# Attention and two feed-forwards on one core: part of the gate products moved to VectorE, weight jobs in other slots, and a new order of the prologue

## The chip, the cores and the metric

The kernel runs on one core of a Trainium2 chip. A core has TensorE (PE, matrix products; PEld is its weight load), VectorE (DVE), ScalarE (ACT), GpSimd (POOL) and SyncE (SP), each with an instruction stream of its own, run in order; a stream stands still where an instruction waits for a semaphore. Matrix products land in PSUM banks, 128 partitions by 512 float32; all other tiles lie in SBUF. Transfers are issued by SP, ACT or POOL and carried by 16 DMA engines. The metric is the device time of one launch in microseconds (us), the median of several runs.

## The reference

Batch 4, 8 heads, 576 tokens, head size 64. Two attentions are added: one over tokens averaged by four (144 by 144, repeated back to 576), one over a band in which positions differ by under four. Their sum, 2304 tokens by 512 channels, goes through two feed-forwards:

```python
out_up = np.repeat(sm_attn(q_d, k_d, v_d), 4, axis=2)        # q_d, k_d, v_d: means of 4 tokens
mask = np.abs(pos[:, None] - pos[None, :]) < 4
out_local = np.matmul(softmax(where(mask, scores, -1e9)), v)
x = (out_up + out_local), as 2304 x 512
x = relu(x @ w_in) ** 2 @ moe_w_out                          # hidden 2048
return (x @ w_a) * (x @ w_b) @ moe2_w_out                    # hidden 1536
```

## The kernel before

**Operands in two halves.** Each float32 operand of the feed-forwards is split in a high part (a copy to fp32r, by `copy` L126 to L128 or `split` L777) and a low part, the rest (`subtract`, L774, or `low`, L179). A product takes three matmuls: high by high, high by low, low by high. A first-feed-forward weight comes through these steps, named as in the order string: wd (load, L143), wr (`rescale`), ws (`shorten`, L158 on VectorE or L126 on ScalarE), wa (`assemble`, L164 and L169, always VectorE), wh (high), wl (low).

**Prologue, 0 to about 124 us.** The attention of the first tiles, the first weights and the first feed-forward tiles are issued in the order of the string `ORDER`; the loop over its tokens stands at the end of that part. A token is a name, numbers, and a letter for the engine (A ScalarE, V VectorE, G GpSimd, S SyncE) or for the PSUM pool (a, h, x, y) that the step uses. b? are steps of the local attention of blocks 0 and 1 on PE (bq the load of q, k and mask; bs scores; bm the mask by L491; bn normalised; bh and bl high and low of the finished block), p? those of the pooled attention (pc and po copies out of PSUM), w? the weights; H is a hidden tile (12 matmuls of 128x256, L589), J its relu, square and high, L its low (`g`, L603), P its projection (L610).

**First feed-forward, to 546.7 us.** 9 tiles of 256 tokens by 16 hidden blocks. During it the other attention tiles run, on DVE, POOL and ACT.

**Second feed-forward, hidden, 546.7 to 819.8 us.** Two spans of 1024 tokens and a rest of 256; the hidden blocks are taken in six pairs j. Spans use a seven-product scheme for 2x2 blocks, the list `ORDER7`: each of its rows is for w = 0, 1 (w_a, w_b) six matmuls of 128x512 (`chain`, L914) into one of the bank pairs X, V, Y. After rows r1, r2 and C22, ScalarE copies X into r1, r2, r3 (L1006); after C11, C22, C21 `plus` (L963, VectorE) adds Y or V to r1, r3, r2, and `product` (L966, POOL) multiplies the a half and the b half, which is the gate product. The results, with c (L1015, L1017) and the differences t5, t7, t6, t4, are stored in y_d by SP (L960).

**Slots.** Before each w of a row, `next_slot` runs the side jobs of that slot: 32 slots for a j, 14 for a span and 4 for the rest tiles. A weight job, `Pair`, has 11 steps, one a slot, from its slot on: a or b prepares a pair of w_a or w_b for the next j; o prepares a pair of the output weights, whose 8 blocks (`wos`, from a pool of six buffers) are split by ScalarE (L854) and POOL, and stored by SP in wo_d (L857). A job's load is put in the slot where the job before last ended. SP works in order, and has eight semaphores for its transfers, DMAHW0 to DMAHW7, used in turn.

**Output, 819.8 to 951.5 us.** `out_span` takes 84 operands `op`, made by `make` from the stored y: high by ScalarE (L777), low by VectorE (L774). `make_to(n)` makes them up to the n-th; the first four are made in slot 26 of the last j.

Of the kernel before, what the change touches and what calls it, by code (L numbers as in the profile page):

```python
# [40 lines left out]
bt.1.0.0.x be.1.1 wr.4.G wa.2 pq.0.A bt.0.1.0.a bt.0.1.1.a ws.4.V.h bc.1.0.0.A bc.0.1.0.A ws.3.V.y bc.0.1.1.A
wa.3 ps.0.0.1.a wh.2.A bd.1.1 ps.0.1.0.a pa.0.1.2 ps.0.0.0.a wl.2.G bn.1.1.V px.0.1.0 bt.1.0.1.h wh.3.A px.0.0.0
pe.0.0.0 pe.0.1.0 ws.5.V.y wh.1.V bw.0.1.x bw.0.0.h px.0.0.1 bt.1.1.0.a wa.4 pe.0.0.1 bt.1.1.1.h ps.0.1.1.a
ps.0.2.0.a pd.0.0 wl.1.V wl.3.G pn.0.0.G wh.4.V px.0.1.1 pt.0.0.1.h bo.0.0.A ps.0.3.0.a wr.5.V bc.1.1.0.A wd.7.S
bv.1.S pa.0.1.3 wr.7.V bo.0.1.A wa.5 wd.9.A pt.0.0.0.h px.0.2.0 px.0.3.0 pe.0.1.1 pd.0.1 bw.1.0.h bc.1.0.1.A
pc.0.0.1.A bc.1.1.1.A wl.4.G wh.5.A ps.0.2.1.a pc.0.0.0.A wr.9.G bw.1.1.y wr.6.V ps.0.3.1.h wd.8.S wd.10.A
bo.1.0.A pe.0.3.0 px.0.2.1 ws.6.V.h pe.0.2.0 ws.7.A.h pe.0.2.1 wl.5.V wa.6.b pn.0.1.G wr.10.G pd.0.2 wh.6.A
pn.0.2.V bo.1.1.A px.0.3.1 wa.7 wd.11.A pw.0.0.a pt.0.2.0.y ws.9.A.- wl.6.V wd.13.A pt.0.2.1.a pt.0.1.0.x
po.0.0.V pe.0.3.1 pc.0.2.1.A wr.11.V pc.0.2.0.A pw.0.2.y pt.0.1.1.h pd.0.3 wh.7.A wr.8.V po.0.2.A ws.8.A.h
wl.7.G wa.8 pn.0.3.G pt.0.3.0.a pc.0.1.0.V ws.10.A.a pc.0.1.1.A pw.0.1.a ws.11.A.y ba.0.0.G ba.1.0.G wa.10.b  # L50
pt.0.3.1.x pc.0.3.1.A pc.0.3.0.A wh.8.A pw.0.3.h pl.1 wr.13.V pa.1.0.0 bh.0.0.V wa.11 wd.12.S po.0.1.A wa.9.-
pa.1.0.1 po.0.3.A wh.9.A ws.13.A.y pa.1.1.0 bl.0.0.V wl.8.G wh.11.V pa.1.0.2 wa.13 ba.0.1.G wl.9.V bh.0.1.A
bl.0.1.G wh.10.A H.0 wh.13.A H.1 wl.13.G ws.12.V.a wr.12.A wd.14.S wr.14.G wl.10.V J.0 wd.19.A wd.16.S wa.12.b
ws.14.A.a bh.1.0.G L.0 J.1 H.2 pa.1.1.1 wa.14.- wr.16.A bl.1.0.G wh.12.A wl.11.V ba.1.1.V wd.15.S wh.14.A H.3
P.0 wd.18.S bh.1.1.V wd.17.A wl.14.V ws.16.A.a wl.12.V J.2 wr.15.A J.3 L.1 wa.16 P.1 L.2 ws.15.A.a wh.16.A H.4
J.4 P.2 bl.1.1.G H.5 wr.18.V wr.17.V ws.17.V.a wa.15.b wa.17.b pa.1.0.3 H.6 H.7 pq.1.A wd.20.S L.3 ps.1.0.0.a
wh.15.A ws.18.V wr.19.V wr.20.A wl.15.V L.4 wh.17.A ws.19.A.a pa.1.1.2 wa.18.- wd.21.S J.5 wd.23.S wl.17.V
wr.21.A ws.20.A.a ps.1.0.1.a wa.19.- L.5 wd.22.A wl.16.G wh.18.G H.8 wr.23.G wa.20 px.1.0.1 wd.24.S P.3 H.9 P.4
J.6 L.6 wr.22.A ws.21.V P.5 wd.25.S J.7 P.6 wh.20.A px.1.0.0 wa.21.- wl.18.G wh.21.V pe.1.0.0 wh.19.G pa.1.1.3
ws.24.A J.8 wl.19.V L.7 ps.1.2.0.a wr.24.V pe.1.0.1 ws.22.V.h wa.22.b ws.23.A.a L.8 wh.22.A pd.1.0 wr.25.A  # L60
pn.1.0.A wa.23.b ps.1.1.0.a wl.21.G px.1.1.0 wd.28.S wr.28.V wl.22.V wl.20.G wd.29.S wd.27.S P.7 pt.1.0.0.a
wh.23.A wa.24.- wl.23.V H.10 wh.24.A J.9 ws.25.A.h wr.27.V H.11 wl.24.G L.9 P.8 pe.1.1.0 pc.1.0.0.V ps.1.1.1.a
wa.25 wd.26.A P.9 ws.28.A.a wa.28 wd.30.S ws.27.A.h J.10 wh.25.A wr.29.V ws.29.V.- wl.25.G wd.31.S wh.28.V L.10
J.11 P.10 wa.27.b wh.27.A pt.1.0.1.h wr.26.A wl.27.V wa.29.- ws.26.A.a wa.26.- wr.31.A L.11 wl.28.G wh.29.G
px.1.1.1 H.12 pc.1.0.1.A J.12 wh.26.A wl.26.G H.13 ws.31.A.h pw.1.0.a wa.31.b pe.1.1.1 L.12 P.11 J.13 po.1.0.V
wr.30.A ws.30.A.h L.13 wa.30 pd.1.1 wl.29.G wh.30.G pn.1.1.A wl.30.G wh.31.A P.12 H.14 J.14 wl.31.V P.13 H.15
J.15 L.14 pt.1.1.0.a H.16 J.16 L.15 L.16 H.17 J.17 P.14 P.15 H.18 J.18 H.19 J.19 L.18 L.17 P.16.xy H.20 L.19
J.20 L.20 P.17 P.18 P.19 H.21 J.21 H.22 J.22 P.20 H.23 J.23 H.24 J.24 L.22 L.21 L.24 P.21 H.25 J.25 L.23 P.22
H.26 J.26 P.23 L.26 H.27 P.24 J.27 L.25 H.28 L.27 P.25 J.28 H.29 P.26 J.29 H.30 L.29 L.28 P.27 J.30 H.31 J.31
P.28 L.31 L.30 P.29  # L70
# [1243 lines left out]
```

## Time and profile before

| what | us |
| --- | --- |
| median of 3 runs (lowest, highest) | 960.22 (959.61, 962.17) |
| profiled execution | 957.15 |
| its span | 955.4 |
| PE, DVE, ACT, POOL busy in the span | 895.9, 699.2, 498.8, 439.2 |
| mean granted clock, as a share of full speed | 0.982 |

A profile row gives, by engine, line and operation, `out<-in`, the shape and a count. In a timeline the first two numbers are start and duration, and [x <-e] at the end says that the engine stood x us before it and that e released it. Successive operations overlap a little, so a group's duration is less than the sum.

### The profile page before, as it was taken

To read this page: it belongs to the slowest core of one execution; us is meant where nothing else is said; L and a number is where in the kernel's file an instruction comes from. 1 tells how busy PE (TensorE), PEld (TensorE's weight loads), DVE (VectorE), ACT (ScalarE), POOL (GpSimd) and SP (SyncE) were. 2 spreads that over 40 slices of the span, in tenths; PEclk is the share of its full clock that TensorE was granted. 3 is DMA by queue.
4 is the path that set the end of the run, shared out by engine and by line. 5 is a ranking of instruction groups with operands and counts; after the bars stand their busy time and mean duration, and the time that the engine had idled before them with its cause. 6 is when DMAs were issued, how large, how long until landed. Compare 5 with 4: busy or idle time off the path is not lost.

```text
span 955.4 us, 16577 instructions
## 1 busy us (share of the span) xinstructions
PE 895.9 (94%) x6128; PEld 812.3 (85%) x6128; DVE 699.2 (73%) x957; ACT 498.8 (52%) x1272; POOL 439.2 (46%) x378
## 2 busy tenths in 40 slices
...
GB/s 295 210 192 239 249 82 80 174 124 71 61 93 211 57 82 49 73 82 68 94 63 127 130 38 134 252 262 178 232 201 221 224 206 288 411 404 404 242 97 80
DMA packets 69889, 161.89 MB, mean 169 GB/s; under 512 B 8472, under 2 KB 16920, under 8 KB 69808
## 3 DMA queue, kind: packets, MB, share of 16 engines
...
q10 hardware_dynamic: 2304, 7.43, 2.2%
q8 instruction: 48, 0.79, 0.3%
...
HBM read 115.71 MB, written 45.09 MB: 168 GB/s over the span
## 4 chain that ended last, share of the span: by engine, by line
PE 71%; DVE 9%; POOL 8%; DMA 6%; issue 3%; ACT 3%; SPq 0%; ACTq 0%; POOLq 0%; DVEq 0%
PE bank L914 35%; PE bank L610 17%; PE bank L589 16%; DMA raw<-in_w_in 3%; POOL pv L418 2%; DVE pv L409 2%; POOL pv L417 2%; DMA qkd<-in_qk_p 1%; PE bank L250 1%; DVE raw L169 1%; DVE xb L774 1%; PE bank L312 1%; DVE bank L164 1%; DVE w L179 1%; DMA band<-in_mask 1%
## 5 line engine op out<-in xcount | busy, mean ns | idle before, releaser
L589 PE MATMUL bank<-xx,w 128*128 128x256 f32 x1728 | 236.4, 287 | 5.3 <-ACT xx L126 2.6
L610 PE MATMUL bank<-g,w 128*128 128x256 f32 x1728 | 234.2, 286 | 6.6 <-DVE g L603 6.6
L914 PE MATMUL bank<-xb,wb 128*128 128x512 f32 x1008 | 234.0, 392 | 5.7 <-ACT r L1006 4.7
L914 PEld LDWEIGHTS bank<-xb,wb 128*128 128x128 f32 x1008 | 189.0, 189 | 48.6 <-ACT r L1006 8.0
L589 PEld LDWEIGHTS bank<-xx,w 128*128 128x128 f32 x1728 | 221.7, 195 | 7.8 <-ACT xx L126 2.9
L610 PEld LDWEIGHTS bank<-g,w 128*128 128x128 f32 x1728 | 216.7, 192 | 12.6 <-DVE g L603 7.4
L914 PE MATMUL bank<-op,wo 128*128 128x512 f32 (+1 forms) x648 | 131.7, 365 | 0.0
L417 POOL TENSOR_TENSOR pv<-pv 128x768 f32<-128x768 f32 x28 | 53.2, 1900 | 168.4 <-DVE pv L409 168.4
L914 PEld LDWEIGHTS bank<-op,wo 128*128 128x128 f32 x648 | 112.0, 189 | 19.7
L597 ACT ACTIVATE bank<-bank 128x256 f32<-128x256 f32 x144 | 53.1, 369 | 136.4 <-PE bank L589 135.8
L774 POOL TENSOR_TENSOR wb<-raw,wb 128x256 fp32r<-128x256 f32 x96 | 93.8, 998 | 34.1 <-ACT wb L854 30.3
L603 DVE TENSOR_TENSOR g<-bank,g 128x256 fp32r<-128x256 f32 x144 | 59.2, 418 | 63.0 <-ACT g L600 62.5
L409 DVE TENSOR_TENSOR pv<-vt,sc 128x1792 f32<-128x1792 f32 x28 | 82.7, 2957 | 19.4 <-POOL x L420 19.3
L966 POOL TENSOR_TENSOR r<-r 128x512 f32<-128x512 f32 x36 | 54.6, 1516 | 59.3 <-DVE r L963 40.3
L774 DVE TENSOR_TENSOR op<-ys,op 128x512 fp32r<-128x512 f32 x84 | 54.9, 713 | 32.3 <-ACT op L777 32.3
L1006 ACT ACTIVATE r<-bank 128x512 f32<-128x512 f32 x72 | 42.8, 595 | 65.5 <-PE bank L914 59.3
L963 DVE TENSOR_TENSOR r<-bank,r 128x512 f32<-128x512 f32 x72 | 48.4, 683 | 30.3 <-PE bank L914 20.1
L777 ACT ACTIVATE op<-ys 128x512 fp32r<-128x512 f32 x84 | 47.1, 624 | 24.3 <-DMA ys<-y_d 13.1
L126 ACT ACTIVATE raw<-raw 128x512 uint32<-128x512 uint32 (+1 forms) x87 | 53.3, 671 | 11.7 <-DMA raw<-in_w_in 9.9
L369 DVE TENSOR_TENSOR p<-qt,kt 128x1792 f32<-128x1792 f32 x28 | 59.1, 2109 | 0.0
L600 ACT ACTIVATE g<-bank 128x256 fp32r<-128x256 f32 x144 | 55.3, 384 | 4.6
L418 POOL TENSOR_TENSOR pv<-pv 128x256 f32<-128x256 f32 x28 | 55.5, 1984 | 2.2
...
## 6 DMA issues: line engine op xcount, KB each, us to landing
...
```

The lines of the kernel that those rows point to most:

```text
L126: engine.activation(out=out, in_=in_, func=AF.Copy, scale=scale)
L369: nc.vector.tensor_tensor(out=self.p, in0=q.unsqueeze(2).to_broadcast([P, FACTOR, WIN, D]), in1=window(k), op=ALU.mult,)
L409: nc.vector.tensor_tensor(out=p, in0=window(heads.pop(("v", n))), in1=self.s[:, :, h].unsqueeze(3).to_broadcast([P, FACTOR, WIN, D]), op=A ...
L417: add(out=p[:, :, 0:3], in0=p[:, :, 0:3], in1=p[:, :, 3:6], op=ALU.add)
L418: add(out=p[:, :, 0], in0=p[:, :, 0], in1=p[:, :, 1], op=ALU.add)
L589: nc.tensor.matmul(out=h, lhsT=wi[f].w[:, a, ct * P:(ct + 1) * P], rhs=x_rhs(i, ct, b), start=(n == 0), stop=(n == 3 * NCT - 1),)
L600: nc.scalar.activation(out=self.g[:, 0], in_=h, func=AF.Copy)
L603: nc.vector.tensor_tensor(out=self.g[:, 1], in0=self.h, in1=self.g[:, 0].bitcast(F32), op=ALU.subtract)
L610: nc.tensor.matmul(out=x2[et // 2][:, et % 2 * T1:(et % 2 + 1) * T1], lhsT=wo[f].w[:, a, et * P:(et + 1) * P], rhs=g[:, b], start=(f == 0 ...
L774: engine.tensor_tensor(out=out, in0=in0, in1=in1, op=ALU.subtract)
L914: nc.tensor.matmul(out=out, lhsT=blk[:, a, cols:cols + P], rhs=rhs[b], start=(start and n == 0), stop=(stop and n == 2), skip_group_check= ...
L966: nc.gpsimd.tensor_tensor(out=r[n][:, 0], in0=r[n][:, 0], in1=r[n][:, 1], op=ALU.mult)
```

## The change

1. `ORDER` is written anew. Block 1's load (bq.1.A) comes first; steps go to other engines, above all off VectorE (ws.2 and ws.6 to ScalarE, bn.1.1 and wl.5 to GpSimd, bh.0.0 and po.0.0 to ScalarE) and some to it (wr.2, pc.0.0.1, pc.0.2.0, wl.8). Two new tokens, Z.0.1.a and Z.7.1.a, each do one 128x128 transpose of the identity into a bank that nothing reads.
2. For r1 and r2, `plus` for w = 1 leaves its sum in the bank and VectorE multiplies from there: 24 of the 36 gate products. r3's 12 stay on POOL.
3. The jobs' slots are a list, `JOBS`: letter, pair, and slot counted over all six j. It read before, in the same form: a1.10 b1.18 o0.28 a2.37 o1.45 b2.54 a3.64 o2.74 b3.85 a4.96 o3.106 b4.117 a5.128 o4.138 b5.149 o5.160.
4. In the last j, the loads of output weights take other slots, and the first four operands are made in slot 31, the last, instead of 26.

```diff
-bq.0.S bs.0.0.0.x bs.0.1.0.a wd.1.A bs.0.0.1.a bm.0.0.0 bm.0.0.1 ws.1.A.- pl.0 bq.1.A wd.0.A bm.0.1.0 bs.1.0.1.y
+bq.1.A bq.0.S bs.0.0.0.x wd.1.A bm.0.0.0 pl.0 bs.1.0.1.y bs.0.0.1.h bs.0.1.0.x bm.0.0.1 ws.1.A.- wd.0.A bm.0.1.0
...
+JOBS = """
+a1.11 b1.18 o0.29 a2.34 o1.47 b2.54 a3.64 o2.74 b3.86 a4.96 o3.105 b4.116 a5.127 o4.138 b5.150 o5.160
+"""
...
+    def warm(_, n, kind):
+        s = bank(kind)
+        for _ in range(n):
+            nc.tensor.transpose(s[:, :P], ident, ident)
+
     acts = {
+        "Z": warm,
...
-    for j in range(NP):
-        at = {0: (10, 18, 28), 1: (5, 13, 22), NP - 1: (0, 0, 0)}.get(j, (0, 10, 21))
-        for n, name in enumerate("aob" if j else "abo"):
-            if name == "o" or j + 1 < NP:
-                jobs.append((SLOTS * j + at[n], Pair(sources[name], name, j + (name != "o"))))
+    for job in JOBS.split():
+        at, name, j = int(job[3:]), job[0], int(job[1])
+        jobs.append((at, Pair(sources[name], name, j)))
...
         def plus(n, w, b):
-            nc.vector.tensor_tensor(out=r[n][:, w], in0=bk[b, w], in1=r[n][:, w], op=ALU.add)
-
-        def product(n, key):
-            nc.gpsimd.tensor_tensor(out=r[n][:, 0], in0=r[n][:, 0], in1=r[n][:, 1], op=ALU.mult)
+            out = bk[b, w] if w and n != "r3" else r[n][:, w]
+            nc.vector.tensor_tensor(out=out, in0=bk[b, w], in1=r[n][:, w], op=ALU.add)
+
+        def product(n, key, b):
+            if n == "r3":
+                nc.gpsimd.tensor_tensor(out=r[n][:, 0], in0=r[n][:, 0], in1=r[n][:, 1], op=ALU.mult)
+            else:
+                nc.vector.tensor_tensor(out=r[n][:, 0], in0=bk[b, 1], in1=r[n][:, 0], op=ALU.mult)
...
-    put(base + 12, [lambda: load_wo("A11", range(NP)), lambda: load_wo("A22", (0, 1))])
-    put(base + 19, [lambda: load_next(8)])
-    put(base + 20, [lambda: load_wo2("S3", (0, 2, 4))])
-    put(base + 22, [lambda: load_wo2("S2", (0, 2, 4))])
+    put(base + 11, [lambda: load_wo("A11", range(NP)), lambda: load_wo("A22", (0, 1))])
+    put(base + 20, [lambda: load_next(8)])
+    put(base + 17, [lambda: load_wo2("S3", (0, 2, 4))])
+    put(base + 27, [lambda: load_wo2("S2", (0, 2, 4))])
...
-        put(base + 22 + 2 * n, [lambda key=key, j=j: load_wo(key, (j, j + 1))])
-    put(base + 26, [lambda: make_to(1), lambda: make_to(2), lambda: make_to(3), lambda: make_to(4)])
+        put(base + 21 + 2 * n, [lambda key=key, j=j: load_wo(key, (j, j + 1))])
+    put(base + 31, [lambda: make_to(1), lambda: make_to(2), lambda: make_to(3), lambda: make_to(4)])
```

The lines of the kernel are counted differently after it: L126 becomes L130, L143 L147, L459 to L465 become L463 to L469, L774 L785, L854 L865, L857 L868, L960 L969, L963 L975, L1006 L1021, L1015 L1031, L1017 L1033; VectorE's product is L981.

**ScalarE, the start of the program.** Before, with the loads of w_in (raw), block 1's q, k and mask (qb, kb, band) and a weight's shorten (the ACTIVATE on raw):

```order
L143 DMA raw<-in_w_in 128x1024
L126 ACT_TABLE_LOAD
L126 ACTIVATE raw<-raw 128x512 [waits DMAHW0_49]
L459 DMA qb<-in_q_t 128x1024
L463 DMA kb<-in_k_t 128x524 x2
L465 DMA band<-in_mask 128x140 [waits DMAHW2_49]
L143 DMA raw<-in_w_in 128x1024 [waits DMAHW4_49]
```

And the same place in the new order:

```order
L463 DMA qb<-in_q_t 128x1024
L467 DMA kb<-in_k_t 128x524 x2
L469 DMA band<-in_mask 128x140
L147 DMA raw<-in_w_in 128x1024
L130 ACT_TABLE_LOAD
L130 ACTIVATE raw<-raw 128x512 [waits DMAHW5_49]
L147 DMA raw<-in_w_in 128x1024 [waits DMAHW4_49]
```

Block 1's four transfers moved ahead of the first weight's load and of the ACTIVATE that waits for it.

**ScalarE, second feed-forward, second span of j = 1, about 620 to 634 us of the trace of before.** r is the copy out of bank X, wos a block of an output weight, raw the rescale or shorten of a weight. Before:

```order
L854 ACTIVATE wos<-raw 128x256 [waits DMAHW2_49]
L1006 ACTIVATE r<-bank 128x512 [waits DMAHW7_49,PE_49]
L854 ACTIVATE wos<-raw 128x256 [waits DMAHW4_49]
L1006 ACTIVATE r<-bank 128x512 [waits PE_49]
L854 ACTIVATE wos<-raw 128x256 [waits DMAHW1_49,DVE_49,Pool_49]
L854 ACTIVATE wos<-raw 128x256 [waits DVE_49]
L854 ACTIVATE wos<-raw 128x256 [waits DMAHW5_49,Pool_49]
L126 ACTIVATE raw<-raw 128x512 [waits DMAHW2_49]
L126 ACTIVATE raw<-raw 128x512
L1006 ACTIVATE r<-bank 128x512 [waits DMAHW4_49,DMAHW7_49,DVE_49,PE_49]
L854 ACTIVATE wos<-raw 128x256 [waits DMAHW0_49,Pool_49]
```

The same place in the new order:

```order
L865 ACTIVATE wos<-raw 128x256 [waits DMAHW0_49,DVE_49]
L1021 ACTIVATE r<-bank 128x512 [waits DMAHW1_49,PE_49]
L865 ACTIVATE wos<-raw 128x256 [waits DMAHW2_49,DVE_49]
L1021 ACTIVATE r<-bank 128x512 [waits PE_49]
L865 ACTIVATE wos<-raw 128x256 [waits DMAHW3_49]
L865 ACTIVATE wos<-raw 128x256 [waits DMAHW4_49]
L865 ACTIVATE wos<-raw 128x256 [waits DVE_49,Activation_49]
L130 ACTIVATE raw<-raw 128x512 [waits DMAHW0_49,Pool_49]
L130 ACTIVATE raw<-raw 128x512
L1021 ACTIVATE r<-bank 128x512 [waits DMAHW3_49,DMAHW7_49,DVE_49,PE_49]
L865 ACTIVATE wos<-raw 128x256 [waits DMAHW6_49,DVE_49,Pool_49]
```

The third r copy of these rows, which opens r2, stands behind seven of the job's blocks before (the last five shown) and behind five now; the raw ahead of it belongs to the b job, whose load moved up.

**SP, the same place: loads of w_b (raw), stores of y and of output blocks (wos).** Before:

```order
L143 DMA raw<-in_w_o 128x1024 [waits DMAHW6_49]
L960 DMA y_d<-r 128x512 [waits DMAHW7_49,Pool_49]
L960 DMA y_d<-r 128x512 [waits DMAHW0_49,Pool_49]
L857 DMA wo_d<-wos 128x512 [waits DMAHW1_49,Pool_49]
L143 DMA raw<-in_w_b 128x1024 [waits DMAHW2_49,DVE_49]
L143 DMA raw<-in_w_b 128x1024 [waits DMAHW3_49]
L960 DMA y_d<-r 128x512 [waits DMAHW4_49,DVE_49]
```

In the new order:

```order
L147 DMA raw<-in_w_o 128x1024 [waits DMAHW6_49]
L969 DMA y_d<-r 128x512 [waits DMAHW7_49,DVE_49]
L147 DMA raw<-in_w_b 128x1024 [waits DMAHW0_49,Pool_49]
L147 DMA raw<-in_w_b 128x1024 [waits DMAHW1_49,Pool_49]
L969 DMA y_d<-r 128x512 [waits DMAHW2_49,Pool_49]
L969 DMA y_d<-r 128x512 [waits DMAHW3_49,DVE_49]
L969 DMA y_d<-r 128x512 [waits DMAHW4_49,DVE_49]
```

The load of w_b moved ahead of the first output block's store, and the stores of r1 and r2 wait for DVE where they waited for Pool.

**VectorE, from the last hidden span into the output stage.** c is the product in the C12 row, r<-bank `plus`, r<-c, r<-r,c and t<-r the differences t5, t7 and t6, op<-ys the low half of an output operand. Before:

```order
L774 TENSOR_TENSOR op<-ys,op 128x512 [waits DMAHW0_49,Activation_49]
L774 TENSOR_TENSOR op<-ys,op 128x512 [waits Activation_49]
L1017 TENSOR_TENSOR c_9277<-bank,c_9277 128x512 [waits DMAHW6_49,DMAHW5_49,PE_49]
L774 TENSOR_TENSOR r<-c_9277,r 128x512 [waits DVE_49,Pool_49]
L963 TENSOR_TENSOR r<-bank,r 128x512 [waits DMAHW3_49,DMAHW1_49,PE_49]
L774 TENSOR_TENSOR r<-r,c_9277 128x512 [waits Pool_49]
L963 TENSOR_TENSOR r<-bank,r 128x512 [waits PE_49]
L774 TENSOR_TENSOR t_9315<-r 128x512 [waits DMAHW6_49,DVE_49]
L774 TENSOR_TENSOR r<-r,t_9315 128x512 [waits DVE_49,Pool_49]
```

In the new order:

```order
L1033 TENSOR_TENSOR c_9270<-bank,c_9270 128x512 [waits DMAHW5_49,DMAHW6_49,PE_49,Activation_49]
L785 TENSOR_TENSOR r<-c_9270,r 128x512 [waits DVE_49]
L975 TENSOR_TENSOR r<-bank,r 128x512 [waits DMAHW3_49,PE_49]
L785 TENSOR_TENSOR op<-ys,op 128x512 [waits DMAHW2_49,Activation_49]
L785 TENSOR_TENSOR r<-r,c_9270 128x512 [waits Pool_49]
L975 TENSOR_TENSOR bank<-bank,r 128x512 [waits PE_49]
L981 TENSOR_TENSOR r<-bank,r 128x512 [waits DVE_49]
L785 TENSOR_TENSOR op<-ys,op 128x512 [waits Activation_49]
L785 TENSOR_TENSOR t_9311<-r 128x512 [waits DMAHW6_49,DMAHW0_49]
L785 TENSOR_TENSOR op<-ys,op 128x512 [waits DMAHW3_49,Activation_49]
L785 TENSOR_TENSOR op<-ys,op 128x512 [waits Activation_49]
```

The four op rows stood ahead of c (the last two of them shown); now the first stands behind the first `plus` and the second behind the product, in the middle of the last tile's work.

## Rows read from the trace of the kernel before

**Rows 1.** Windows of the prologue: window, length, busy time of each engine, PEclk, DMA share, GB/s.
```profile
20.00:40.00 20.00, 8.18 (x64) 6.50 (x65) 16.73 (x33) 15.18 (x64) 10.14 (x9) 1.00 0.74 185
40.00:60.00 20.00, 13.37 (x175) 10.39 (x171) 18.36 (x36) 14.26 (x48) 10.47 (x9) 0.79 0.77 232
60.00:80.00 20.00, 13.21 (x66) 10.94 (x67) 17.10 (x26) 10.85 (x24) 15.68 (x19) 0.52 0.81 218
80.00:100.00 20.00, 16.86 (x122) 15.86 (x121) 18.39 (x36) 12.57 (x29) 10.68 (x11) 0.91 0.79 209
100.00:124.00 24.00, 21.72 (x178) 20.29 (x176) 22.17 (x41) 19.32 (x52) 7.80 (x7) 1.00 0.64 223
```

**Rows 2.** Windows of the second feed-forward: PE, PEld, DVE, ACT, POOL, PEclk, DMA share, GB/s.
```profile
560.00:600.00 40.00, 37.80 (x208) 31.78 (x207) 39.62 (x54) 22.57 (x50) 26.27 (x23) 1.00 0.34 112
628.00:635.00 7.00, 4.49 (x20) 3.42 (x19) 2.38 (x3) 2.76 (x6) 5.42 (x7) 1.00 1.00 363
640.00:680.00 40.00, 40.00 (x201) 34.06 (x200) 34.63 (x45) 22.73 (x50) 32.70 (x31) 1.00 0.60 212
```

**Rows 3.** Timeline of PE, second feed-forward, 599 to 645 us: start, duration, instruction.
```profile
599.87 5.63 PE L914 MATMUL bank<-xb,wb 128*128 128x512 f32 x24
606.27 1.66 PE L914 MATMUL bank<-xb,wb 128*128 128x512 f32 x6 [0.77 <-ACT r L1006]
608.18 23.61 PE L914 MATMUL bank<-xb,wb 128*128 128x512 f32 x102 [0.24 <-ACT r L1006]
634.30 10.26 PE L914 MATMUL bank<-xb,wb 128*128 128x512 f32 x36 [2.52 <-ACT r L1006]
```

**Rows 4.** Timeline of VectorE in the prologue.
```profile
16.67 0.81 DVE L491 SCALAR_TENSOR_TENSOR blk<-bank,band 128x280 f32<-128x280 f32 x2 [5.31 <-DMA band<-in_mask]
...
30.65 0.68 DVE L158 TENSOR_SCALAR bank<-raw 128x512 uint32<-128x512 uint32 x1
...
43.08 0.42 DVE L128 CAST w<-raw 128x512 fp32r<-128x512 f32 x1
...
63.44 0.67 DVE L128 CAST xx<-xb 128x256 fp32r<-128x256 f32 x2
```

**Rows 5.** Timeline of ScalarE and its DMA issues (ACTq) at the start.
```profile
6.14 0.65 ACT L126 ACTIVATE raw<-raw 128x512 uint32<-128x512 uint32 x1 [3.69 <-DMA raw<-in_w_in]
6.15 0.33 ACTq L459 DMA_DIRECT2D qb<-in_q_t  x1
```

**Rows 6.** Timeline of PE at the first feed-forward's start.
```profile
73.11 7.87 PE L589 MATMUL bank<-xx,w 128*128 128x256 f32 x41 [0.35 <-POOL xx L571]
80.81 1.72 PE L610 MATMUL bank<-g,w 128*128 128x256 f32 x13
```

**Rows 7.** Chain that ended last, where the second feed-forward starts: start, duration, what.
```profile
546.89 6.84 PE bank L914 x30
```

**Rows 8.** Timeline of ScalarE, 626 to 635 us.
```profile
632.24 0.43 ACT L854 ACTIVATE wos<-raw 128x256 fp32r<-128x256 f32 x1 [5.02 <-DMA wo_d<-wos]
...
633.67 0.58 ACT L1006 ACTIVATE r<-bank 128x512 f32<-128x512 f32 x1
```

**Rows 9.** Timeline of SP's DMA issues, the same stretch.
```profile
626.79 2.67 SPq L960 DMA_DIRECT2D y_d<-r  x2
```

**Rows 10.** Timeline of POOL: two gate products.
```profile
561.24 1.68 POOL L966 TENSOR_TENSOR r<-r 128x512 f32<-128x512 f32 x1 [4.24 <-DVE r L963]
...
627.44 1.67 POOL L966 TENSOR_TENSOR r<-r 128x512 f32<-128x512 f32 x1 [2.07 <-DVE r L963]
```

**Rows 11.** All instructions of line 1017: shortest, median, longest in ns; first and last start.
```profile
L1017 DVE TENSOR_TENSOR c<-bank,c x12: 675/679/692, 570.6 to 818.2; 128x512 f32<-128x512 f32 x12
```

**Rows 12.** Timeline of VectorE, 557 to 564 us: differences of two SBUF tiles.
```profile
557.48 1.28 DVE L774 TENSOR_TENSOR x2s<-x2s 128x512 f32<-128x512 f32 x2
...
561.08 2.38 DVE L774 TENSOR_TENSOR x2s<-x2s 128x512 f32<-128x512 f32 x2
```

**Rows 13.** Timeline of PE at the start of the output stage.
```profile
819.84 6.51 PE L914 MATMUL bank<-op,wo 128*128 128x512 f32 x28
```

More of the change, by code (lines that the diff above doesn't have):

```diff
@@ L41 @@
[L41 to L70, printed above, removed]
+bq.1.A bq.0.S bs.0.0.0.x wd.1.A bm.0.0.0 pl.0 bs.1.0.1.y bs.0.0.1.h bs.0.1.0.x bm.0.0.1 ws.1.A.- wd.0.A bm.0.1.0
@@ new lines @@
+bx.0.0 be.0.0 pf.0.0.2 pa.0.1.0 Z.0.1.a pf.0.0.3 bs.0.1.1.a pa.0.0.0 pa.0.1.1 pa.0.0.1 wd.6.S wd.2.A pf.0.1.2
+wr.1.V bm.1.0.1 bs.1.0.0.y wr.0.A bs.1.1.0.h bm.0.1.1 wd.3.S pf.0.1.3 bm.1.0.0 ws.0.A.h bd.0.0 bx.0.1 wd.5.S
+wa.0.b wh.0.V wl.0.V wr.3.G be.0.1 bs.1.1.1.x bx.1.0 bd.0.1 bm.1.1.1 bn.0.1.G ws.2.A.h wd.4.A pj.0.1.G wa.1.b
+bm.1.1.0 be.1.0 wr.2.V bn.0.0.V bt.0.0.0.h bt.0.0.1.y bd.1.0 pj.0.0.V pq.0.A bc.0.0.0.A bn.1.0.G bx.1.1 bv.0.S
+be.1.1 wr.4.G bt.1.0.0.x bc.0.0.1.V bt.0.1.0.a bt.0.1.1.a ws.3.V.h ps.0.1.0.a bc.0.1.0.A ws.4.V.h wa.2
@@ new lines @@
+bc.0.1.1.A wa.3 pa.0.1.2 wh.2.A bd.1.1 ps.0.0.1.a bc.1.0.0.A wl.2.G ps.0.0.0.h bn.1.1.G px.0.1.0 bt.1.0.1.h
+px.0.0.0 ws.5.V.y wh.3.A wh.1.V bw.0.1.x bw.0.0.h px.0.0.1 pe.0.0.0 wa.4 bt.1.1.1.a bt.1.1.0.a pe.0.0.1 wl.1.V
+ps.0.1.1.a pd.0.0 pe.0.1.0 wl.3.G wh.4.V px.0.1.1 bo.0.0.A pn.0.0.G ps.0.3.0.a pt.0.0.1.h ps.0.2.0.a bc.1.1.0.A
+wr.5.V wa.5 wd.7.S pa.0.1.3 bv.1.S px.0.3.0 bo.0.1.A wd.9.A pt.0.0.0.h wr.7.V pe.0.1.1 bw.1.0.h bc.1.0.1.A
+px.0.2.0 ps.0.3.1.h pc.0.0.1.V wl.4.G pc.0.0.0.A pd.0.1 bc.1.1.1.A wh.5.A wd.8.S ps.0.2.1.a bo.1.0.A wr.9.G
@@ new lines @@
+wr.6.V wd.10.A px.0.2.1 bw.1.1.a ws.6.A.h pe.0.2.0 ws.7.A.h pe.0.2.1 pe.0.3.0 wl.5.G pn.0.1.G wa.6.b pd.0.2
+wh.6.A pw.0.0.a pn.0.2.V bo.1.1.A pt.0.1.0.x px.0.3.1 Z.7.1.a wa.7 wd.11.A wr.10.A ws.9.A.- wr.11.V po.0.0.A
+wd.13.A pt.0.2.0.y pt.0.2.1.a pe.0.3.1 pc.0.2.1.A wr.8.V pc.0.2.0.V ws.8.A.h pw.0.2.y pd.0.3 wh.7.A pt.0.1.1.h
+po.0.2.A wr.13.V wl.7.G pn.0.3.G pt.0.3.0.a pc.0.1.0.V pc.0.1.1.A wa.8 pt.0.3.1.h pw.0.1.a ba.0.0.G wl.6.V
+ws.10.A.a ws.11.A.y wh.8.A pc.0.3.1.A pc.0.3.0.A bh.0.0.A wl.8.V ba.1.0.G pw.0.3.h pl.1 pa.1.0.0 wa.10.b
@@ new lines @@
+po.0.1.A wa.11 wd.12.S pa.1.0.1 wa.9.b bl.0.0.V ws.13.A.y po.0.3.A wh.9.A bh.1.0.A wl.9.V pa.1.1.0 wh.10.A
+pa.1.0.2 wa.13 ba.0.1.G ws.12.V.a bh.0.1.A wh.11.V bl.0.1.G H.0 wd.16.S wh.13.A H.1 wl.13.G wr.12.A J.0 wd.14.S
+wl.10.V H.2 wa.12.b ws.14.A.a wr.14.G wr.16.A wd.19.A wa.14.- pa.1.1.1 wh.14.A L.0 wh.12.A bl.1.0.G wd.18.S
+ba.1.1.V J.1 wl.11.V wd.15.S H.3 P.0 bh.1.1.V wd.17.A wl.14.V ws.16.A.a J.2 ws.15.A.a L.1 wr.15.A H.4 wa.16 J.3
+wr.18.V wl.12.V L.2 wh.16.A bl.1.1.G H.5 wr.17.V wd.20.S P.1 wd.23.A ws.17.V.a L.3 J.4 wa.15.b wa.17.b pa.1.0.3
```

23 lines of the change are left out of this document (17 added, 6 removed).

## The prediction

> **What bounds the kernel now.** I read the granted clock and the slices first, then the busy time of each engine in windows, then the waits of TensorE (PE), then the timelines of the engines around those waits. The profiled execution took 957.15 us (span 955.4 and 1.75 around it); the median of the runs is 960.22, so I work out differences on the trace and put them on the median.
>
> In the prologue, PE is not the limit. From 20 to 100 us it works 8.18, 13.37, 13.21 and 16.86 of each 20 us, and VectorE (DVE) 16.73, 18.36, 17.10 and 18.39; from 100 to 124 PE has nearly caught up, 21.72 of 24 [rows 1]. So up to there an instruction taken off VectorE is worth about its duration, if data come no later: the 16 DMA engines are 0.64 to 0.81 busy in the same windows. Further on PE fills its time but for two places. In 560 to 600 it works 37.80 of 40 while VectorE works 39.62 [rows 2]. In the second feed-forward's hidden spans around 600 to 645 PE stands still before ScalarE's copy of r: 0.77, 0.24 and 2.52 us [rows 3].
>
> **The change part by part.**
>
> *Prologue, engines.* I compared the two strings token by token. Up to the first hidden tile (H.0) VectorE loses ws.2 and ws.6 (a shorten each, 0.68), bn.1.1 and wl.5 (0.68 each, priced as a shorten), po.0.0 (0.42, priced as the plain copy), and bh.0.0 (two halves, 0.67); it gains wr.2, pc.0.0.1 and pc.0.2.0 (0.42 each) and wl.8 (0.68) [rows 4]. That is 4 x 0.68 + 0.42 + 0.67 = 3.81 less 3 x 0.42 + 0.68 = 1.94: -1.87 us. After H.0 it loses wh.21, wr.28, po.1.0 (0.42 each) and wl.19 (0.68) and gains wr.20 (0.42): -1.52. Together **-3.4**. ScalarE (15.18, 14.26, 10.85, 12.57 of 20) and GpSimd (10.14, 10.47, 15.68, 10.68) [rows 1] have room for what they are given.
>
> *Prologue, loads.* Block 1's q, k and mask stand behind ws.1 on ScalarE, which waits 3.69 us for its weight; so they are issued from 6.15 us on, and VectorE later stands 5.31 us, until 16.67, for that mask [rows 4, 5]. In the new order ScalarE issues them first and the weight behind them. At best the 5.3 us of idle go. But the DMA engines are shared: the weight, which all of wa.1 hangs on, and block 0's own loads on SP now run beside 1.1 MB more (qb 512 KB, two kb of 262, a mask of 70), which at the 210 to 230 GB/s of rows 1 is 5 us. I take 0, between -5.3 and +5, since VectorE's idle moves rather than goes when the bytes stay the same. The Trainium skill ("Trainium Kernel Development and Optimization", Key Constraints) says that DMAs from the SP, ACT and POOL queues share the same 16 engines, and that issuing from several saves issue time only; by it alone this edit brings at most the issue wait, and my 0 stands.
>
> *Idle transposes.* Two PE instructions of 128x128. The first 41 hidden matmuls take 7.87 / 41 = 0.19 us each [rows 6], so two such cost 0.4 at most, and the PE idle of 11.82 us in 20 to 40 hides them. They also take a turn of a PSUM pool, so that later tiles meet other banks, which no row prices: 0, from -0.4 to +0.4. In 60 to 80 the granted clock is 0.52, near the lower of its two levels (1.2 of 2.4 GHz) [rows 1], and those 41 run in it; the 13 after them take 1.72 / 13 = 0.13 each [rows 6]. With the full clock there 41 x 0.06 = 2.5 us would go. One transpose at the start and one before that stretch are little work, and I give the clock nothing in the sum.
>
> *FFN2, 599.87 to 644.56.* A matmul of 512 columns takes 6.84 / 30 = 0.228 us when PE has no wait (the stage's first 30). There are 24 + 6 + 102 + 36 = 168 of them in 44.69 us; 168 x 0.228 = 38.3, so 6.4 us are lost [rows 3, 7]. Where the 2.52 go can be followed back: ScalarE's r copy stands in order behind a split of an output block (wos) that cannot start until 632.24, 5.02 us after its last work, for the store of an earlier block [rows 8]. Those stores go through the SP queue, and SP stood 2.67 us at y stores [rows 9], of which one waited for GpSimd's product, 627.44 to 629.11 [rows 10]; the DMA engines are at 1.00 with 363 GB/s [rows 2]. Behind the 2.52 come 36 matmuls of 0.285 instead of 0.228: 2.0 us at a lower clock. In the new order three things change here. The r copy stands ahead of the first block that needs a store of its own job to have ended, behind five blocks and not seven. The in_w_b load is issued ahead of the stores. And SP's y stores of r1 and r2 wait for VectorE, not GpSimd, whose 24 products (1.67 the one in rows 10) are gone. So the 2.52 + 0.2 should go, and with it the 2.0, and the losses at 606.27 (0.77 + 0.24 of gaps) partly: the first output job only moves from slot 28 to 29, and its store burst stays. I keep 1.4 of the 6.4: **-5.0**, between 0 and -6.4.
>
> *Products on VectorE.* A product with one operand in a bank is like the c product: 0.68 us [rows 11]. There are 24, 16.3 us of VectorE time. From 560 to 600 VectorE is at 39.62 of 40 and gets four: +2.7. Against this, VectorE's operations with two SBUF operands are slow beside a GpSimd product: a pair of x2s differences takes 1.28 alone and 2.38 while one runs, from 561.24 on [rows 10, 12], 1.1 us back for each product that leaves. Four of those would be -4.4. I take 0, from -1.7 to +2.7. After 640, where PE is busy without a gap and VectorE has 5.4 of 40 us free [rows 2], they cost nothing. The Trainium skill ("SBUF — State Buffer", Who interferes with whom) says that only the port pair shared by VectorE and GpSimd contends, held by one at a time, and that VectorE uses it for a second SBUF operand; the two durations agree.
>
> *Boundary at 819.84.* Here PE begins the output stage [rows 13]. Before, VectorE has made the low halves of the first four operands by then. In the new order, as their splits move from slot 26 to 31, they stand after the last hidden tile's work: plus w0, low of operand 0, t7, plus w1, product, low of operand 1. Bank V's first half is ready 6 x 0.228 = 1.4 us before 819.84, at 818.47; six instructions of 0.68 end at 822.55. PE wants operand 1's low after four matmuls, at 819.84 + 0.91 = 820.75. It stands **+1.8** us. At a pitch of 0.60 (1.28 - 0.68 in rows 12) it is 1.3; if the clock drops after the gap as it did behind the 2.52, 1.8 + 2.0 = 3.8.
>
> *Job slots and loads elsewhere.* From 640 on PE has no gap [rows 2], so shifts by a slot change nothing: 0.
>
> Sum: -3.4 - 5.0 + 1.8 = **-6.6**: 948.8 for the span, 950.55 for the execution, 953.6 on the median.
>
> **Rivals.** R1, the prologue gains nothing: the engines' time is set by the loads (share 0.74 to 0.81 [rows 1]), so VectorE waits where it worked. For it: the mask that VectorE waits for. Against: VectorE is 84 to 92% busy. -5.0 + 1.8 = -3.2: 957.0. R2, slower: VectorE becomes the bound in the second feed-forward. Seven more products from 560 to 640 (two a span of 84 x 0.228 = 19.2 us, with 5 us of rest tiles between spans of two blocks) are 7 x 0.68 = 4.8 on the path, because VectorE has 0.4 us free in 560 to 600 [rows 2] and no relief is felt; in 600 to 645 the stores stay the limit (0), and the prologue gives 0 by R1's reason, with the boundary at +1.8: +6.6, 966.8; with half of the prologue's gain 965.1. It decides once a product costs more than the relief it gives. R3, the stores stay the limit: the DMA engines are full there [rows 2], an earlier in_w_b load only moves bytes; prologue -3.4, FFN2 -1.0, boundary +1.8: -2.6, 957.6. R4, a larger gain: the half clock at the first hidden tiles goes too (-2.5) and all 6.4 come back: -3.4 - 2.5 - 6.4 + 1.8 = -10.5: 949.7.
>
> **How the numbers follow.** Forecast 0.45 (its own range 950 to 957), R1 0.18, R3 0.13, R2 0.12, R4 0.12. About 0.3%, 2.9 us, can be told from no change. Faster: 0.41 of the forecast, R4's 0.12, 0.10 of R1 and 0.04 of R3, 0.67; same: 0.04 of the forecast, 0.08 of R1 and 0.09 of R3, 0.21; slower: R2's 0.12. The range of 947.5 to 962 holds the forecast, R1, R3 and most of R4, and leaves out R2 and the ends of R4.
>
> **What would show it.** In the new profile: first steady hidden tiles some 3 us sooner, and VectorE's share in 20 to 100 no higher; in the stretch from the rest tiles to 645 no wait of PE for ScalarE's r over 1 us, and ScalarE no longer standing 5 us at a wos; VectorE products of 0.68, and x2s pairs near 1.28; at the boundary a wait of PE for an op low of 1.3 to 3.8 us. Wrong would be: the same start of full PE use (R1), PE waiting for VectorE's r between 555 and 640 (R2), or the wos wait still there (R3).

## The result and the profile after

The changed kernel takes 952.4 us (median of 5, 949.38 to 955.47), the kernel before 961.02 in the same comparison; the ratio is 0.9911, 95% interval [0.9892, 0.9931], which is 8.6 us, where 6.6 were forecast. A second comparison gave 0.9915 [0.9892, 0.9937]. The profiled execution took 949.86, its span is 948.1: 7.3 less than before. The table splits the span at four points of PE's timeline: the first matmul of the second feed-forward, the first of its second pair's spans, the first of that pair's rest tiles, and the first of the output stage. The times in brackets are those of the kernel before:

| stage, us of the trace | before | changed | difference | forecast |
| --- | --- | --- | --- | --- |
| to the second feed-forward | 546.73 | 544.44 | -2.29 | -3.4 |
| first part, to the second pair's spans (599.87) | 53.14 | 52.30 | -0.84 | 0 |
| from there to the second pair's rest tiles (644.40) | 44.53 | 38.39 | -6.14 | -5.0 |
| from there to the output stage (819.84) | 175.44 | 175.44 | 0.00 | 0 |
| output stage, to the span's end | 135.56 | 137.53 | +1.97 | +1.8 |

Timeline of PE in the changed kernel, second feed-forward and start of the output stage (as [rows 3, 13]); the numbers are start and duration:

```profile
544.44 16.51 PE L925 MATMUL bank<-xb,wb 128*128 128x512 f32 x72
561.47 3.46 PE L925 MATMUL bank<-xb,wb 128*128 128x512 f32 x12 [0.52 <-DVE r L975]
...
576.68 1.66 PE L925 MATMUL bank<-xb,wb 128*128 128x512 f32 x6 [0.53 <-ACT r L1021]
...
596.74 38.56 PE L925 MATMUL bank<-xb,wb 128*128 128x512 f32 x168
635.13 5.92 PE L925 MATMUL bank<-xr,wb 128*128 128x256 f32 x48
...
810.57 1.17 PE L925 MATMUL bank<-op,wo 128*128 128x512 f32 x4
813.31 46.99 PE L925 MATMUL bank<-op,wo 128*128 128x512 f32 x206 [1.57 <-DVE op L785]
```

The 168 matmuls that took 44.69 us from the first start to the last end, with four starts, are one piece of 38.56 now: 0.23 each, the rate of [rows 7]. The 2.52 and the slow 36 behind it are both gone. At the other end PE does four matmuls and stands 1.57 us for VectorE's low half of the second operand; from its first matmul to its fifth it takes 2.74 us, where four at 0.228 take 0.91.

ScalarE and SP in the same place, the second span of the second pair, changed kernel (as [rows 8, 9]):

```profile
621.79 0.44 ACT L865 ACTIVATE wos<-raw 128x256 fp32r<-128x256 f32 x1 [1.82 <-DVE raw L857]
622.13 1.23 ACT L130 ACTIVATE raw<-raw 128x512 f32<-128x512 f32 x2
623.26 0.57 ACT L1021 ACTIVATE r<-bank 128x512 f32<-128x512 f32 x1
623.74 0.42 ACT L865 ACTIVATE wos<-raw 128x256 fp32r<-128x256 f32 x1
...
```

```profile
615.99 4.24 SPq L969 DMA_DIRECT2D y_d<-r  x3
620.33 0.38 SPq L868 DMA_DIRECT2D wo_d<-wos  x1
622.33 0.32 SPq L969 DMA_DIRECT2D y_d<-t  x1
622.74 0.88 SPq L868 DMA_DIRECT2D wo_d<-wos  x2
```

The wos ahead of the r copy now waits 1.82 us, for a weight from VectorE. From 590 to 650 us none of ScalarE's splits waits for a store of output blocks in this profile (one does in the second, 1.1 us); after 650 such waits come to 1.9 us, and PE has no gap there. SP still stands 4.24 at y stores with the stores of output blocks behind them, but no wait of ScalarE for these follows here. The windows say the same: PE without a gap, and VectorE busier than the 29.95 of 40 it had before in 600 to 640.

```profile
560.00:600.00 40.00, 38.53 (x212) 32.56 (x211) 39.13 (x59) 24.05 (x54) 21.45 (x23) 1.00 0.47 164
600.00:640.00 40.00, 40.00 (x196) 33.65 (x195) 36.57 (x51) 23.76 (x53) 28.34 (x30) 1.00 0.74 265
```

The products themselves: all 24 of VectorE, in ns (shortest, median, longest), and a pair of x2s differences with no product on POOL beside it (as [rows 12], where it was 2.38).

```profile
L981 DVE TENSOR_TENSOR r<-bank,r x24: 691/692/693, 558.9 to 812.0; 128x512 f32<-128x512 f32 x24
...
559.53 1.28 DVE L785 TENSOR_TENSOR x2s<-x2s 128x512 f32<-128x512 f32 x2
```

In the prologue (as [rows 1]) VectorE is less busy in 20 to 40 than before, 13.07 where it was 16.73, and PE too; the run of 41 hidden matmuls starts at 73.84, later than the 73.11 of [rows 6].

```profile
20.00:40.00 20.00, 6.91 (x33) 5.26 (x34) 13.07 (x28) 12.07 (x53) 9.31 (x8) 1.00 0.72 187
...
60.00:80.00 20.00, 14.03 (x78) 11.38 (x79) 16.89 (x28) 13.30 (x28) 14.33 (x17) 0.55 0.77 197
...
100.00:124.00 24.00, 22.57 (x182) 21.32 (x180) 23.32 (x43) 21.40 (x58) 10.90 (x10) 1.00 0.68 228
```

### The profile page after: what moved, and what is told of

The parts are those of the page before. It is cut to its first block, busy times and chain, and to the rows that moved or that the text cites. A ratio compares the mean times of both kernels' runs of the same rounds, so it can differ in the third digit from the quotient of the medians.

```text
span 948.1 us, 16541 instructions
## 1 busy us (share of the span) xinstructions
PE 895.6 (94%) x6130; PEld 813.0 (86%) x6130; DVE 692.6 (73%) x975; ACT 503.4 (53%) x1280; POOL 391.8 (41%) x352
## 4 chain that ended last, share of the span: by engine, by line
PE 77%; DVE 7%; POOL 6%; DMA 6%; issue 2%; ACT 2%; ACTq 0%; SPq 0%; DVEq 0%; POOLq 0%
PE bank L925 39%; PE bank L614 17%; PE bank L593 16%; DMA more<-in_qk_p 2%; POOL pv L422 2%; DVE pv L413 2%; DMA qkd<-in_qk_p 2%; POOL pv L421 2%; PE bank L254 1%; DMA raw<-in_w_in 1%; PE bank L316 1%; DMA raw<-in_w_out 1%; DVE xb L785 1%; POOL x L424 1%; POOL pv L423 1%
## 5 line engine op out<-in xcount | busy, mean ns | idle before, releaser
L925 PE MATMUL bank<-xb,wb 128*128 128x512 f32 x1008 | 231.3, 390 | 1.5 <-ACT r L1021 0.8
L785 POOL TENSOR_TENSOR wb<-raw,wb 128x256 fp32r<-128x256 f32 x96 | 88.3, 941 | 55.8 <-ACT wb L865 49.6
L1021 ACT ACTIVATE r<-bank 128x512 f32<-128x512 f32 x72 | 42.8, 595 | 73.4 <-PE bank L925 71.9
L785 DVE TENSOR_TENSOR op<-ys,op 128x512 fp32r<-128x512 f32 x84 | 54.0, 708 | 31.3 <-ACT op L788 31.3
L130 ACT ACTIVATE raw<-raw 128x512 uint32<-128x512 uint32 (+1 forms) x87 | 53.2, 669 | 9.7 <-DMA raw<-in_w_in 7.4
L785 POOL TENSOR_TENSOR wos<-raw,wos 128x256 fp32r<-128x256 f32 x48 | 46.2, 982 | 28.8 <-ACT wos L865 25.7
L382 DVE TENSOR_REDUCE sc<-p 128x28 f32<-128x1792 f32 x28 | 56.2, 2007 | 0.0
```

The lines of the kernel that those rows point to most:

```text
L130: engine.activation(out=out, in_=in_, func=AF.Copy, scale=scale)
L382: nc.vector.tensor_reduce(out=self.s[:, :, h], in_=self.p, axis=AX.X, op=ALU.add)
L785: engine.tensor_tensor(out=out, in0=in0, in1=in1, op=ALU.subtract)
L925: nc.tensor.matmul(out=out, lhsT=blk[:, a, cols:cols + P], rhs=rhs[b], start=(start and n == 0), stop=(stop and n == 2), skip_group_check= ...
```

## The experiments

Each is measured against the kernel before on the same chip, in 5 rounds. Order, products, job slots and both ran on one chip; slot 26 (first time), no idle transposes, block 1's load late and the moves back on a second; the changed kernel again, slot 26 again, block 1's load first and the moves alone on a third. Times from different chips are compared by their ratios to the kernel before.

**Order alone.** The new `ORDER` and `warm` in the kernel before.

```diff
-bq.0.S bs.0.0.0.x bs.0.1.0.a ...
+bq.1.A bq.0.S bs.0.0.0.x wd.1.A ...
+        "Z": warm,
```

> The kernel before with the new prologue order alone (both idle transposes in it). Theory (the gains of the three parts add up, each in its own stage): the first feed-forward ends 2.3 us sooner, as in the changed kernel, and everything behind it is as before, the wait of TensorE for ScalarE's r of 2.5 us near 632 included: 960.2 - 2.3 = 957.9 to 958.7. Rival (the new order only pays together with the rest, or its gain was the luck of one profile): within 1 us of before, 960 to 962.

Measured: 955.23, ratio 0.9951 [0.9934, 0.9968], 4.7 us less (3.1 to 6.3). The second feed-forward starts at 544.62, and the stage is no better than before:

```profile
604.66 1.66 PE L920 MATMUL bank<-xb,wb 128*128 128x512 f32 x6 [1.25 <-ACT r L1012]
...
633.32 10.26 PE L920 MATMUL bank<-xb,wb 128*128 128x512 f32 x36 [3.12 <-ACT r L1012]
```

So the prologue's gain is its own. It is larger than the 2.29 of the two profiles; the profile of before was at the good end, for its 957.15 lies under the 959.61 of the fastest of the five runs behind the median. With the old prologue the second feed-forward starts at 546.73, 549.26, 548.22 and 549.73 in four profiles (before and the next three kernels), with the new one at 544.44, 544.62, 543.13, 544.62 and 548.18 in five. The means are 548.5 and 545.0, and the spread is wide: 543.13 and 548.18 are two profiles of one program, the one with slot 26 below. They come apart above all between 109 and 122 us: one group of four transposes starts at 109.17 in the one and at 110.42 in the other, a later one at 118.11 and 121.74. From 112 to 116 PE is busy throughout in both, with the granted clock at 1.00 in the first and at 0.50, the lower level, in the second.

**Products alone, job slots alone, and both.** The two parts of the second feed-forward in the kernel before.

```diff
+            out = bk[b, w] if w and n != "r3" else r[n][:, w]          # products
+                nc.vector.tensor_tensor(out=r[n][:, 0], in0=bk[b, 1], in1=r[n][:, 0], op=ALU.mult)
...
+    for job in JOBS.split():                                           # job slots
```

> The kernel before with the 24 gate products of r1 and r2 on VectorE alone. Theory A (the y stores that waited for GpSimd's product, and with them the output blocks' stores behind, made ScalarE late): the wait of 2.5 us near 632 shrinks to under 1 and the second feed-forward's hidden stage is 3 to 5 us shorter, 956 to 958. Theory B (the slots of the weight jobs do it, the products only move work): the waits in 600 to 645 stay at 2.5 us or more, VectorE in 560 to 600 is at the limit of 40 us and adds up to 2.7: 960 to 963.

> The kernel before with the new slots of the weight jobs alone. Theory B (the earlier load of w_b and the r copy that stands ahead of the first output block that needs a store of its own job): most of the 6.1 us of 600 to 645 go, 954.5 to 956. Theory A (GpSimd's products hold SP's stores up): under 2 us of them go, 959 to 961.

> The kernel before with both, the products on VectorE and the new job slots; the order of the prologue and the place of the first four output operands as before. If the parts add up: the hidden stage is 7.0 us shorter as in the changed kernel, and TensorE has no wait of 1.6 us at the start of the output stage: 953.5 to 954.5. If the early place of the operands (slot 26) costs in the last hidden span what it saves at the boundary: 955 to 956.

Measured, with ScalarE's waits for output blocks' stores in 590 to 650 us of each trace; the hidden stage runs from the first matmul of the second feed-forward to the first of the output stage, and the column of the 168 matmuls goes up to the start of the rest tiles:

| kernel | median, ratio [95%] | hidden stage | its part to the second pair | 168 matmuls | ScalarE, wos for wo_d |
| --- | --- | --- | --- | --- | --- |
| before (profile) | - | 273.11 | 53.14 | 44.53 | 12.6 |
| products | 957.07, 0.9974 [0.9963, 0.9985] | 270.66 | 53.46 | 41.76 | 5.7 |
| job slots | 956.36, 0.9972 [0.9957, 0.9987] | 270.55 | 53.81 | 41.30 | none |
| both | 953.16, 0.9936 [0.9922, 0.9950] | 266.86 | 52.26 | 39.16 | none |

Rows of the waits from before, from the products alone, and from the job slots alone: who waited for what, us in total, times, longest.

```profile
ACT wos L854 <- DMA wo_d<-wos: 12.6, 4, 5.0
```

```profile
ACT wos L854 <- DMA wo_d<-wos: 5.7, 4, 2.1
```

```profile
ACT wos L857 <- DVE raw L172: 5.2, 4, 2.6
...
POOL r L967 <- DVE r L964: 10.9, 4, 5.1
PE bank L917 <- DVE r L964: 1.6, 1, 1.6
```

Both theories hold in part, and neither alone: 2.5 and 2.6 us of the stage each, 6.2 together. That the parts help one another is likely and not certain: the excess, some 1.2 us, is less than the 1.6 by which the stage differs in the four profiles with the old products and slots (272.62 to 274.24). The products halve the stores' wait, and PE's wait for the r copy is down to 0.93 and 0.43, but it then stands 1.21 for VectorE. The slots remove the stores' wait, and PE waits 1.61 us for VectorE's `plus`; VectorE is busy 14.79 of the 15 us from 630 to 645 there (as it is in the changed kernel, where PE does not wait). With both, 0.74 of that wait is left. Which move in the slots did it, the r copy's place or the earlier load of w_b, no run separates. The gain of 6.1 us (4.8 to 7.5) by time fits the 6.25 of the trace, and "both" has no wait at the start of the output stage.

**First operands in slot 26**, in the changed kernel, twice; the second time beside the changed kernel itself.

```diff
-    put(base + 31, [lambda: make_to(1), lambda: make_to(2), lambda: make_to(3), lambda: make_to(4)])
+    put(base + 26, [lambda: make_to(1), lambda: make_to(2), lambda: make_to(3), lambda: make_to(4)])
```

> The changed kernel with the first four output operands made in slot 26 again. Theory: their low halves are ready before the output stage, the wait of TensorE for the second operand's low (1.57 us) goes, and nothing else moves: 1.6 us less than the changed kernel's 952.4, 950 to 951.5. Rival: made in slot 26 they sit in front of the last span's copies and sums, and TensorE waits there for as long: 952 to 953.

> The changed kernel itself, once more, beside the next three on one chip. Its 5 runs so far span 949.4 to 955.5, the second feed-forward took 266.1 us in its profile against 266.9 in four relatives. Expected: a ratio to before of 0.989 to 0.993, the spread of some 5 us again, and a first feed-forward that ends between 543 and 549.

> The changed kernel with the first four output operands in slot 26, beside the changed kernel on one chip. Theory (the 1.57 us at the output stage's start are pure loss): 1.5 to 2 us below the changed kernel of this comparison. Rival (given back in the last span): the same within 0.7. The profile decides it more sharply than the time: from the start of the second feed-forward to the end of the span 402.4 us against the changed kernel's 403.7 or more.

Measured: 949.86, 0.9913 [0.9888, 0.9937]; and 948.33, 0.9896 [0.9873, 0.9920] beside 950.61, 0.9915 [0.9892, 0.9937] for the changed kernel. The intervals overlap, so the times alone do not tell them apart. The profiles do: from the start of the second feed-forward to the end of the span it is 402.4 us in both profiles (543.13 to 945.5, 548.18 to 950.6) and 404.4 for the changed kernel beside it (544.62 to 949.0), 403.7 in its first profile, and 404.3 to 404.4 in the three other kernels below with slot 31. The start of the output stage in the changed kernel, second profile, and in the one with slot 26:

```profile
811.49 1.17 PE L925 MATMUL bank<-op,wo 128*128 128x512 f32 x4
814.24 15.96 PE L925 MATMUL bank<-op,wo 128*128 128x512 f32 x69 [1.57 <-DVE op L785]
```

```profile
799.62 15.58 PE L925 MATMUL bank<-xb,wb 128*128 128x512 f32 x68
815.04 15.35 PE L925 MATMUL bank<-op,wo 128*128 128x512 f32 x67
```

No wait, and none that replaces it: from the second pair's rest tiles to the output stage it is 634.55 to 809.99 in the first slot-26 profile, 175.44 us as in the table above. So this version beats the changed kernel too, by 1.3 to 2 us of the trace. The changed kernel's six times spread over some 7 us (948.24 to 955.15), more than the 5 expected. Its second profile has a wait of 0.74 for VectorE at 633.18, which the first lacked; the hidden stage is 266.9 us in it and in the six other profiles with both parts, so the 266.1 of the first was 0.7 of luck.

**No idle transposes**, in the changed kernel.

```diff
-bx.0.0 be.0.0 pf.0.0.2 pa.0.1.0 Z.0.1.a pf.0.0.3 ...
+bx.0.0 be.0.0 pf.0.0.2 pa.0.1.0 pf.0.0.3 ...
...
-... px.0.3.1 Z.7.1.a wa.7 ...
+... px.0.3.1 wa.7 ...
```

> The changed kernel without the two idle transposes. Theory: they are hidden in TensorE's idle time and change nothing, 951.5 to 953.5, the first feed-forward ending within 0.7 us of 544.4. Rival: they change which bank the next tiles get, or the granted clock near 50 to 80 us, and the first feed-forward ends 1 us or more later (954 and over), with a higher or longer half clock in the profile.

Measured: 953.76, 0.9932 [0.9908, 0.9956]. The profile starts the second feed-forward at 548.61, but a run with the transposes in did so at 548.18, and the six times span 948.62 to 956.06. Against 0.9911 to 0.9915 this is 1.6 to 2.0 us, within the noise. It stays open whether they do anything. The granted clock in 60 to 80 is 0.56 without them and 0.55 with; in 100 to 124 it is 0.86 without them and 0.86 as well in the profile that has them and starts at 548.18, against 0.97 to 1.00 in the four profiles that start at 543.13 to 544.62. So the late start comes with the lower clock there, with the transposes or without.

**Block 1's load late**, in the changed kernel, and **first**, in the kernel before. In the late one the step bs.1.0.1.y, which needs this load, moves behind it too.

```diff
-bq.1.A bq.0.S bs.0.0.0.x wd.1.A bm.0.0.0 pl.0 bs.1.0.1.y ... ws.1.A.- wd.0.A bm.0.1.0
+bq.0.S bs.0.0.0.x wd.1.A bm.0.0.0 pl.0 ... ws.1.A.- bq.1.A wd.0.A bm.0.1.0 bs.1.0.1.y
...
-bq.0.S bs.0.0.0.x bs.0.1.0.a wd.1.A ... pl.0 bq.1.A wd.0.A ...
+bq.1.A bq.0.S bs.0.0.0.x bs.0.1.0.a wd.1.A ... pl.0 wd.0.A ...
```

> The changed kernel with block 1's load of q, k and mask (and the one scores step that needs it early) back behind the shorten of the weight, as before. Theory (the bytes are the same and only their order changes): within 1.5 us of the changed kernel, 951 to 954. Rival (the early load is what the new order lives from): the gain of the prologue, some 4 us, goes: 955.5 to 957.5.

> The kernel before with block 1's load of q, k and mask put first, and nothing else changed. Theory (the early load is what the new order lives from): 2 to 4 us less than before, 956 to 957.5 where before is 960. Rival (it only pays with the steps behind it in the new order; the bytes are the same): within 1 us of before, or slower, 959 to 962.

Measured: late 954.82, 0.9944 [0.9926, 0.9963]; first 960.75, 1.0011 [0.9997, 1.0024]. The early load by itself brings nothing, as the prediction had it, and costs 1.1 us if anything. In the new order it is worth about 3 us (0.9944 against 0.9911 and 0.9915; the intervals overlap a little, so this is likely and not certain). In both profiles the 41 hidden matmuls are late, at 76.48 and 76.35; they start at 72.84 to 74.48 in the five profiles with the new order and the early load that have slot 26 or 31 (one of them without the transposes), and at 73.11 to 74.45 in the four with the old prologue. The two results fit a match of load and steps that counts, and not the load's place by itself; which steps live from the early load was not separated.

**VectorE's moves back**, in the changed kernel, and **alone**, in the kernel before.

The diff is the first's, six tokens out of five lines of the string; the second has it the other way round.

```diff
-... ws.2.A.h ... bn.1.1.G ... ws.6.A.h ... wl.5.G ... po.0.0.A ... bh.0.0.A ...
+... ws.2.V.h ... bn.1.1.V ... ws.6.V.h ... wl.5.V ... po.0.0.V ... bh.0.0.V ...
```

> The changed kernel with six steps of the prologue given back to VectorE (ws.2, ws.6, bn.1.1, wl.5, po.0.0, bh.0.0; 3.8 us of its time up to the first hidden tile), all else as changed. Theory of the prediction (VectorE bounds the prologue): the first feed-forward ends 2.5 to 3.8 us later, 955 to 956.5. Rival (loads and the order of the steps bound it, VectorE has idle time to put them in): under 1 us, 952 to 953.5.

> The kernel before with the six steps taken off VectorE in the prologue (ws.2 and ws.6 to ScalarE, bn.1.1 and wl.5 to GpSimd, po.0.0 and bh.0.0 to ScalarE), and nothing else changed; 3.8 us of VectorE's time. Theory of the prediction (VectorE bounds the prologue): 2.5 to 3.8 us less than before. Rival, favoured by the run that gave them back: within 1 us of before.

Measured: back 951.92, 0.9925 [0.9904, 0.9945]; alone 958.0, 0.9986 [0.9972, 1.0001]. Alone, 3.8 us of VectorE's time are worth 1.3 us (from -0.1 to 2.7); given back, they cost 1.0 to 1.3, which is within the noise. The best estimate is a third of their duration; nothing at all is not excluded, all of it is. In the profile of the moves alone the hidden matmuls do start sooner, at 71.02, but PE loses it again behind them, and the second feed-forward starts at 547.87, inside the range of the old prologue:

```profile
71.02 8.04 PE L589 MATMUL bank<-xx,w 128*128 128x256 f32 x41 [0.35 <-POOL xx L571]
...
92.56 1.70 PE L589 MATMUL bank<-xx,w 128*128 128x256 f32 x12 [2.45 <-DVE g L603]
```

## Why the prediction was right or wrong

The direction, the size and the places were right: the forecast was 953.6 with 950 to 957 as its own range, the time is 952.4. In the second feed-forward and at the boundary the mechanism was right as well; in the prologue it was not, and its size came out by luck.

*Second feed-forward, 599.87 to 644.56, -5.0.* Right in mechanism, a little small. The stretch is 6.1 us shorter, and the chain from stores over ScalarE to PE is what the job slots and the products each cut (12.6 to 5.7, or to none). The 1.4 us kept back for the first output job's burst was wrong: the wait at 606.27 is gone as well, since ScalarE's waits for wo_d went (12.6 us before, none in one profile and 1.1 in the other). The 2.0 booked to the lower clock did not come with the wait alone: with the products alone the clock is 1.00 over the last 36 matmuls, and from the first of them to the rest tiles they take 10.52 us where they took 10.10, because PE stands 0.43 and 1.21 among them. What came back is the waits of both engines together.

*Products on VectorE, 0.* The price of 0.68 measured 0.692. The relief was real in the one x2s pair that had met a product, 1.28 where it was 2.38, and the part up to the second pair is 0.8 to 0.9 us shorter with products and slots; with either alone it is 0.3 to 0.7 longer. R2 needed a VectorE that gains no relief; in 560 to 600 it is busy 39.13 of 40 and PE gained 0.73 us. R3 needed stores as the limit whatever their order; the DMA share in 600 to 640 stays at 0.74 (0.75 before), with PE full. So it was the order of the stores, not their amount.

*Boundary, +1.8.* The replay held: PE stands 1.57 us behind the end of its fourth matmul, or 1.83 over the 0.91 that four take, for the six instructions of VectorE; the stage is 1.97 longer. It was no trade: slot 26 gives it back and costs nothing.

*Prologue, engines, -3.4.* The step that failed. The sum was near the measured (4.7 by the order alone, 3.1 to 6.3; 2.29 in the two profiles), but not for its reason. "Worth about its duration" was too much: the six moves off VectorE give about 1.3 of their 3.8 us (from -0.1 to 2.7). The steps moved to VectorE and the moves behind the first hidden tile, 1.52 of the 3.4, no run took by themselves. From 90% busy I took VectorE to be on the path all the time, while with less to do it stood longer: 13.07 of 20 in 20 to 40.

So by subtraction most of the gain, some 3 us of 4.7, comes from the order of the steps, with the early load in it, and was not in the prediction: the load was given 0, right alone, but with the steps behind it the new order likely lives from it in part. (Its bound of +5 took the rate of later windows; from 0 to 20 us, where these loads run, 304 GB/s were moved before, by which the 1.1 MB are 3.6 us.) "First steady hidden tiles some 3 us sooner" was wrong for the changed kernel: they start as before (72.84 to 74.48 against 73.11 to 74.45), and the gain comes behind them. PE's last wait of the prologue shows it, 1.43 at 127.31 before and 0.17 at 118.02 in the changed kernel; from 124 to 140 PE works 14.57 of 16 us before and all 16 after. By which tokens was not settled.

*Half clock and idle transposes, 0.* The granted clock in 60 to 80 is 0.55 where it was 0.52, so R4's 2.5 us did not come. R1 falls with the order alone, which is 3.1 to 6.3 us faster.
